# Two DRAM scratch tensors laid out with whole 2 KB rows, their stores split by halves of the partitions

## The chip, the cores and the metric

One NeuronCore of one Trainium2 chip runs the kernel. The metric is device time in microseconds of one launch, as the median of several executions. Each profile is of one execution; its span is the time from the first to the last instruction that the profiler saw.

## The reference, cut to what matters

For a signal `x` of 2048 positions and 512 channels the reference mixes a long convolution (state-space taps `K`, by FFT) and a two-layer MLP with GELU:

```python
g = sigmoid((x * gate_w).sum(-1, keepdims=True))
P = exp(logdA[:, :, None] * l[None, None, :])            # 512 x 128 x 2048
K = einsum("dn,dnl,dn->dl", Cc, P, dB).real              # the taps
y = irfft(rfft(pad(x.T)) * rfft(pad(K)))[:, :2048].T + x * Dskip
b = gelu(x @ w1 + b1) @ w2 + b2                          # F = 1792
return g * y + (1 - g) * b
```

All arrays are float32. The kernel gets `x` in three layouts: `xl` for the transform, `xs` for the gate, `xt` for the MLP.

## The kernel before, in words

The kernel has two stages. The **front** (`front`, lines 347 to 1046) computes the MLP, the taps `K`, and the first step of the Fourier transforms of the signal and of the taps; it lasts until about 406 us. The **convolution stage** (`conv`, lines 1049 to 1233) then finishes the transforms, multiplies them, transforms back and adds everything up.

In the front, TensorE works on three streams. The MLP's products are L870 to L872 (hidden layer, into `ph`, twelve matmuls a block) and L916 to L918 (output layer, into `acc`, three matmuls for each `f`); each product is taken three times, of high and low parts. The taps come in 16 rounds, 4 blocks `u` of channels by 4 parts `c`: VectorE builds powers and rotations (`y`, `xc`), TensorE contracts them (L706), ScalarE copies the result to `s1` (L719), TensorE takes the first transform step (L424, reading `s`), and ScalarE copies that into `sk` (L726). After the fourth part of a block, four DMAs (L745) store `sk` to the DRAM tensor `tk_d`. The signal comes in 16 pieces: a load (L439), the first transform step (L424, reading `attic`), a copy from PSUM (L445 on VectorE for the first three, else L450 on ScalarE) into one of two buffers `st` (a part of `attic`), and a store (L454) of 512 KB to the DRAM tensor `tu_d`.

Both DRAM tensors exist to turn the data: what was stored with frequency and real/imaginary part on the partitions (and channel half `h` on the two halves of the partitions) is read back by `load_u` (L340) and `load_k` (L345) with 64 positions and the two parts on the partitions, and all 512 channels in a row. Each load moves 256 KB; there are 32 of each. Of the `load_u` loads 19 are issued in the front (`early`), the rest and all `load_k` loads in the convolution stage, some steps ahead of their use.

The order of the front is not that of the code. Every step is a task with an engine, an estimated duration, a due time and its reads and writes (`Plan.add`). A planner simulates the engines forwards and backwards 20 times (`Plan.run`), and keeps the order whose simulated end is earliest; the tasks are then issued in that order. The due times come from constants at the head of the file (`K_0`, `D_KA`, `D_S1`, `D_SP`, `D_MAG` and others). So a change of a constant, or of the number of tasks, can move any instruction of the front. DMA tasks go to the SP queue (a few to POOL), which takes them strictly in order: a DMA that waits for its data holds back all DMAs behind it. The `conv` stage has a fixed order.

The convolution stage has 16 steps of about 5.5 us on TensorE: transforms of the taps (`p2k`) and of the signal (`p2u`), both L1090, products on VectorE (L1112 to L1117), and the inverse transform (`pa`, L1129), which goes through DRAM once more (`t4_d`, L1138 and L1147) to the last products `pb` (L1218). Its first step needs a table `cc` (L1062) and the first two `tk` tiles. A `tk` load needs all four last stores of `tk_d`.

Of the kernel before, what the change touches and what calls it, by code (L numbers as in the profile page):

```python
# [9 lines left out]
F32 = mybir.dt.float32  # L10
# [9 lines left out]
D = 512  # L20
# [9 lines left out]
UW = 128  # L30
# [3 lines left out]
NB = 2 * NSB  # L34
T_0 = 19.5
T_MLP = 393.85
K_0 = 27.624
T_KG = 378.228
U_0 = -84.42
U_GAP = 14.351  # L40
LAG = 11.64
D_KA = -51.158
D_KP = -41.862
D_S1 = -7.88
D_EV = -33.69
D_H = -59.76
D_LO = -11.892
N_ACC, N_H, N_IO = 2, 2, 3
D_SP = -9.73
N_LD, N_UX, N_ST = 4, 2, 2  # L50
SCRATCH = 2048
D_XS = 5.631
# [6 lines left out]
W_MLP = (-0.0504, -0.0333, 0.0274)  # L59
W_KG = (-0.054, -0.0194, -0.0114)  # L60
W_U = (-0.0194, -0.1484, 0.0049)
D_MAG = 0.44
D_ROT = 1.203
D_CON = 0.574
D_PHA = 0.94
# [31 lines left out]
def k0_order():  # L97
    return [8 * (n % 4) + n // 4 for n in range(32)]
# [191 lines left out]
def gated_mix(  # L290
# [18 lines left out]
    nc = tc.nc  # L309

    cp = ctx.enter_context(tc.tile_pool(name="cp", bufs=1))
    dr = ctx.enter_context(tc.tile_pool(name="dr", bufs=1, space=DRAM))

    dt_d = dr.tile([1, D], F32, name="dt_d")
    t4_d = dr.tile([4, 2, 2, GROUP, 32, D], F32, name="t4_d")
    tu_d = dr.tile([2, 32, 2, 64, D // 2], F32, name="tu_d")
    tk_d = dr.tile([2, 32, 2, 64, D // UW, 64], F32, name="tk_d")


    ov = out.rearrange("(m i) p d -> m (i p) d", i=2).rearrange("m (p i) d -> m p i d", i=2)  # L320
# [10 lines left out]

        return [attic[:, k] for k in range(N_ATTIC)] + [loft[:, k * D : k * D + D] for k in range(N_LOFT)]

    def halves(z):

        return z.rearrange("p (h e) -> p h e", h=2)

    def load_u(to, n):

        nc.sync.dma_start(halves(to), tu_d[:, k0_order()[n]].rearrange("h c s e -> (c s) h e"))  # L340

    def load_k(to, n):

        of = tk_d[:, k0_order()[n]].rearrange("h c s u e -> (c s) h (u e)")
        nc.sync.dma_start(halves(to), of)  # L345

    def front(pool, psum, keep, attic, loft):

# [17 lines left out]
        def move(kb, fn, due, reads=(), writes=(), queue="SP", after=()):  # L366

            hold = 0.45 if queue == "SP" else 1.0
            return pl.add(queue, hold, fn, due, reads, writes, done=kb / 360.0, after=after)
# [7 lines left out]
        sk = pool.tile([P, 64, NCH, 4, 4], F32, name="sk")  # L377
# [12 lines left out]
        st = [attic[:, 2 * k : 2 * k + 2].rearrange("p a b -> p (a b)").rearrange("p (j e) -> p j e", j=4) for k in range(N_ST)]  # L390
# [38 lines left out]
            mm(1000, products, due + D_S1, [key, "c1"], [("pz", i)], 0.5, switch=True)  # L429
            evac(i)  # L430

        rows = tu_d.rearrange("h k c s e -> (h k c) s e")

        def signal():
            for s in range(16):
                t = U_0 + 16 * U_GAP * warp(s / 16, W_U)
                yield t
                u = s % N_UX
                move(256, lambda s=s, u=u: nc.sync.dma_start(ux[u], xl[s]), t - 10, [], [("ux", u)])  # L439

                def evac(i, s=s, t=t):
                    k = take("st", N_ST)
                    if s < N_SV:
                        vec(
                            4 * 256, lambda: nc.vector.tensor_copy(st[k], pq[i]), t + D_EV,  # L445
                            [("pz", i)], [("st", k)],
                        )
                    else:
                        act(
                            4 * 256, lambda: nc.scalar.copy(st[k], pq[i]), t + D_EV,  # L450
                            [("pz", i)], [("st", k)],
                        )
                    move(
                        512, lambda: nc.sync.dma_start(rows[:, 4 * s : 4 * s + 4], st[k]), t,  # L454
                        [("st", k)], [("u_d", s)],
                    )

                first_stage(lambda r, h, u=u: ux[u][r, 256 * h : 256 * h + 256], ("ux", u), t, evac)
            yield None

        def early():

            us = places(attic, loft)
            keys = [("st", k // 2) for k in range(2 * N_ST)] + [("ux", k) for k in range(N_UX)]
            keys = [*keys, *(("ld", k) for k in range(N_LD)), "gwb"]
            yield 1e6
            for n in range(N_US):
                if n < N_ATTIC:
                    due, key = T_EARLY + 4 * n, [keys[n]]
                else:  # L470
                    due, key = T_LOFT + n, ["xt", "xv"] if n < N_ATTIC + 4 else ["tt"]
                move(
                    256, lambda n=n: load_u(us[n], n), due,
                    [("u_d", k) for k in range(16)], key,
                )
            yield None

# [151 lines left out]
        def waves(t):  # L629
# [4 lines left out]

            act(99 * CW, sines, t + D_KA, ["ph"], ["tt"], "sin", ops=3)

# [18 lines left out]
        e = y[:, 1]  # L655
# [40 lines left out]
        def contract(u, c, k, t):  # L696
# [42 lines left out]
                [("sk", i) for i in range(NCH)],  # L739
            )  # L740
            for h in range(4):
                ss = slice(h * 16, h * 16 + 16)

                def store(ss=ss):
                    nc.sync.dma_start(  # L745
                        tk_d.rearrange("h k c s u e -> (h k c) s u e")[:, ss, u],
                        sk[:, ss].rearrange("p s c j g -> p s (c j g)"),
                    )

                move(700, store, t + 5, [("sk", i) for i in range(NCH)], [])  # L750

        def taps():
# [3 lines left out]
            nth = 0  # L756
            t = K_0
            yield t
# [7 lines left out]
            for g in range(nc_ * NCH):  # L766
                u, c = divmod(g, NCH)
                k = nth % 2
                t = K_0 + T_KG * warp(g / (nc_ * NCH), W_KG)
                yield t  # L770
# [267 lines left out]
        while heap:  # L1038
            heap.sort(key=lambda e: e[:2])
            _, n, s = heap.pop(0)  # L1040
            t = next(s)
# [270 lines left out]
```

## Time and profile before

| what | value |
|---|---|
| median of 3 runs | 535.32 us (534.39 to 537.9) |
| the profiled execution | 536.27 us, span 534.5 us, mean granted TensorE clock 0.979 |
| TensorE (PE) busy | 503.5 us, 94% of the span |
| VectorE (DVE) busy | 426.6 us, 80% |
| ScalarE (ACT) busy | 358.6 us, 67% |
| DMA packets | 90837, 108.61 MB |
| of these under 512 B / under 2 KB | 39056 / 58576 |

Rows of the profile read as follows. A group has source line, engine, operation, `output<-inputs` by the program's tile names, partitions x elements, count, then busy time and the mean of one in ns, and last the idle time of the engine just before these instructions with the one that ended it. A row of a timeline has its start and its length in us. A row of the waits has who waited for whom: us in total, times, longest. A row of a table by windows has, for a stretch `A:B`, the busy us and the count of each engine, then the granted TensorE clock (PEclk, 1.00 is full), the mean busy share of the 16 DMA engines, and what they moved in GB/s. A row of DMA issues has count, KB each and the median us from issue to landing.

### The profile page before, as it was taken

To read this page: it belongs to the slowest core of one execution; us is meant where nothing else is said; L and a number is where in the kernel's file an instruction comes from. 1 tells how busy PE (TensorE), PEld (TensorE's weight loads), DVE (VectorE), ACT (ScalarE), POOL (GpSimd) and SP (SyncE) were. 2 spreads that over 40 slices of the span, in tenths; PEclk is the share of its full clock that TensorE was granted. 3 is DMA by queue.
4 is the path that set the end of the run, shared out by engine and by line. 5 is a ranking of instruction groups with operands and counts; after the bars stand their busy time and mean duration, and the time that the engine had idled before them with its cause. 6 is when DMAs were issued, how large, how long until landed. Compare 5 with 4: busy or idle time off the path is not lost.

```text
span 534.5 us, 11251 instructions
## 1 busy us (share of the span) xinstructions
PE 503.5 (94%) x4426; PEld 352.9 (66%) x4426; DVE 426.6 (80%) x790; ACT 358.6 (67%) x547; POOL 47.3 (9%) x90
## 2 busy tenths in 40 slices
PE   7979999999999799999999999999994899999992
PEld 4757778788777577888788877788783433333360
DVE  5998999989999789999998899997610567666533
ACT  5799887699966898976388968566532454555311
POOL 1000000000000020003110311041001001010103
PEclk9989999999999899999999999999998799999997
DMA  8998923462299269438820547075409979999877
GB/s 254 371 340 308 340 86 117 140 221 66 80 289 304 84 215 279 149 99 219 195 42 2 159 86 152 1 178 89 131 6 217 306 252 312 359 414 385 311 282 288
DMA packets 90837, 108.61 MB, mean 203 GB/s; under 512 B 39056, under 2 KB 58576, under 8 KB 90144
## 3 DMA queue, kind: packets, MB, share of 16 engines
q1 hardware_dynamic: 82944, 87.67, 49.7%
q0 software_dynamic: 7360, 18.65, 14.2%
q10 hardware_dynamic: 480, 1.57, 0.8%
q8 instruction: 35, 0.57, 0.5%
q14 instruction: 18, 0.15, 0.1%
HBM read 62.25 MB, written 45.62 MB: 202 GB/s over the span
## 4 chain that ended last, share of the span: by engine, by line
PE 66%; DVE 11%; DMA 9%; ACT 5%; issue 4%; SPq 2%; POOL 1%; POOLq 0%; DVEq 0%; ACTq 0%
PE pz L706 9%; PE ph L870 7%; PE ph L871 7%; PE ph L872 7%; PE acc L916 6%; PE acc L917 6%; PE acc L918 6%; PE p2k L1090 6%; PE p2u L1090 6%; PE pa L1129 5%; DMA out_dram<-io 2%; PE pz L424 2%; DMA cc<-in_c_dram 1%; DVE y L670 1%; SPq L745 1%
## 5 line engine op out<-in xcount | busy, mean ns | idle before, releaser
L870 PE MATMUL ph<-xh,wh 128*128 128x512 f32 x224 | 90.1, 402 | 0.0
L916 PE MATMUL acc<-wh,hh 128*128 128x512 f32 x210 | 86.0, 410 | 3.4 <-ACT acc L922 2.8
L871 PE MATMUL ph<-xlo,wh 128*128 128x512 f32 x224 | 87.9, 392 | 0.5 <-DVE xlo L804 0.5
L872 PE MATMUL ph<-xh,wl 128*128 128x512 f32 x224 | 87.6, 391 | 0.0
L917 PE MATMUL acc<-wl,hh 128*128 128x512 f32 x210 | 82.7, 394 | 0.0
L918 PE MATMUL acc<-wh,hl 128*128 128x512 f32 x210 | 82.6, 393 | 0.0
L706 PE MATMUL pz<-y,xc 128*32 128x64 f32 x2048 | 61.8, 290 | 5.2 <-ACT attic L450 5.2
L889 ACT ACTIVATE io<-ph,b1t 128x512 f32<-128x512 f32 x56 | 38.6, 689 | 39.2 <-PE ph L872 30.4
L706 PEld LDWEIGHTS pz<-y,xc 128*32 128x32 f32 x2048 | 57.1, 136 | 11.5 <-ACT attic L450 6.1
L898 DVE TENSOR_TENSOR hl<-io,hh 128x512 fp32r<-128x512 f32 x56 | 38.4, 685 | 24.6 <-ACT hh L890 24.6
L916 PEld LDWEIGHTS acc<-wh,hh 128*128 128x128 f32 x210 | 39.7, 189 | 20.1 <-issue 7.1
L870 PEld LDWEIGHTS ph<-xh,wh 128*128 128x128 f32 x224 | 42.3, 189 | 13.8 <-issue 3.8
L871 PEld LDWEIGHTS ph<-xlo,wh 128*128 128x128 f32 x224 | 42.4, 189 | 9.5 <-DVE xlo L804 0.9
L872 PEld LDWEIGHTS ph<-xh,wl 128*128 128x128 f32 x224 | 42.3, 189 | 9.2
L918 PEld LDWEIGHTS acc<-wh,hl 128*128 128x128 f32 x210 | 39.8, 190 | 8.8
L670 DVE TENSOR_TENSOR y<-y,ea 128x64 f32<-128x64 f32 (+4 forms) x80 | 45.2, 565 | 0.4
L1112 DVE TENSOR_TENSOR v<-p2u,k 128x512 f32<-128x512 f32 x16 | 11.1, 691 | 42.5 <-ACT sa L1135 25.3
L917 PEld LDWEIGHTS acc<-wl,hh 128*128 128x128 f32 x210 | 40.0, 190 | 7.5
L515 DVE TENSOR_TENSOR loft<-xc,zz 128x256 f32<-128x256 f32 (+2 forms) x48 | 37.1, 772 | 0.6 <-ACT xc L641 0.5
L516 DVE TENSOR_TENSOR loft<-xc,zz 128x256 f32<-128x256 f32 (+2 forms) x48 | 37.0, 771 | 0.0
L683 DVE TENSOR_TENSOR y<-y,loft 128x2048 f32<-128x2048 f32 x16 | 36.6, 2284 | 0.6 <-ACT loft L633 0.5
L890 ACT CAST hh<-io 128x512 fp32r<-128x512 f32 x56 | 34.8, 622 | 1.8
(139 smaller groups left out, 842.1 us busy)
## 6 DMA issues: line engine op xcount, KB each, us to landing
tu_d<-attic SPq DMA_DIRECT2D x16, 512.0 KB, 4.9
tk_d<-sk SPq DMA_DIRECT2D x16, 512.0 KB, 6.9
tk<-tk_d SPq DMA_DIRECT2D x32, 256.0 KB, 4.9
t_d<-sa SPq DMA_DIRECT2D x31, 256.0 KB, 5.3
t<-t_d POOLq DMA_DIRECT2D x12, 512.0 KB, 7.0
attic<-tu_d SPq DMA_DIRECT2D x22, 256.0 KB, 4.4
attic<-in_xt_dram SPq DMA_DIRECT2D x16, 256.0 KB, 4.1
attic<-in_xl_dram SPq DMA_DIRECT2D x16, 256.0 KB, 4.3
```

Of the source, the lines that this page charges most:

```text
L515: vec(2 * m, lambda: vv.tensor_mul(t, a, br), due, [ka, *kb], [kt])
L670: nc.vector.tensor_mul(both(n, 64 - 3 * n, n), both(0, 64 - n, n), an)
L706: nc.tensor.matmul(pk[32 * j : 32 * j + 32, gg // 4, gg % 4], x[:, r, :, ch], y[:, r, :, ch], start=(r == 0), stop=(r == 1), skip_group_ch ...
L870: nc.tensor.matmul(phs[q], h, xh[d], start=(d == 0), stop=False)
L871: nc.tensor.matmul(phs[q], h, xlo[d], start=False, stop=False)
L872: nc.tensor.matmul(phs[q], lo, xh[d], start=False, stop=(d == 3))
L889: nc.scalar.activation(g, phs[q], AF.Gelu_apprx_tanh, bias=b1t[:, c : c + 1])
L898: SB, lambda: nc.vector.tensor_sub(hl[f], g, hh[f].bitcast(F32)), t + D_LO,
L916: nc.tensor.matmul(a, h, wh[1][f], start=(f == 0 and u >= NSB), stop=False, skip_group_check=True)
L917: nc.tensor.matmul(a, h, wl[1][f], start=False, stop=False, skip_group_check=True)
L918: nc.tensor.matmul(a, l, wh[1][f], start=False, stop=(f == FH - 1), skip_group_check=True)
L1090: nc.tensor.matmul(out[64 * i : 64 * i + 64], w, x, start=True, stop=True)
```

## The change

`tu_d` and `tk_d` get the channel half `h` as an inner dimension instead of the outermost one. In DRAM the two halves of one row (1 KB each) now lie side by side. A load takes 128 contiguous rows of 2 KB instead of 256 pieces of 1 KB. The store of a signal piece, in which `h` lies on the partitions, is now two DMAs of 64 partitions and 256 KB each instead of one of 128 partitions and 512 KB; in DRAM its pieces are 1 KB, every 2 KB, where four of them lay together as 4 KB before. The four stores of a taps block stay four DMAs of 512 KB with pieces of 256 B; each now takes 64 partitions by 32 rows instead of 128 by 16. Five constants of the planner change as well.

```diff
-K_0 = 27.624
+K_0 = 27.09
-D_KA = -51.158
+D_KA = -46.527
-D_S1 = -7.88
+D_S1 = -8.01
-D_SP = -9.73
+D_SP = -13.612
-D_MAG = 0.44
+D_MAG = 0.439
...
-    tu_d = dr.tile([2, 32, 2, 64, D // 2], F32, name="tu_d")
-    tk_d = dr.tile([2, 32, 2, 64, D // UW, 64], F32, name="tk_d")
+    tu_d = dr.tile([32, 2, 64, 2, D // 2], F32, name="tu_d")
+    tk_d = dr.tile([32, 2, 64, 2, D // UW, 64], F32, name="tk_d")
...
     def load_u(to, n):
-        nc.sync.dma_start(halves(to), tu_d[:, k0_order()[n]].rearrange("h c s e -> (c s) h e"))
+        nc.sync.dma_start(to, tu_d[k0_order()[n]].rearrange("c s h e -> (c s) (h e)"))
     def load_k(to, n):
-        of = tk_d[:, k0_order()[n]].rearrange("h c s u e -> (c s) h (u e)")
-        nc.sync.dma_start(halves(to), of)
+        nc.sync.dma_start(to, tk_d[k0_order()[n]].rearrange("c s h u e -> (c s) (h u e)"))
...
-                    move(
-                        512, lambda: nc.sync.dma_start(rows[:, 4 * s : 4 * s + 4], st[k]), t,
-                        [("st", k)], [("u_d", s)],
-                    )
+                    for h in range(2):
+                        def store(h=h):
+                            to = tu_d[:, :, 4 * s : 4 * s + 4, h].rearrange("k c s e -> (k c) s e")
+                            nc.sync.dma_start(to, st[k][64 * h : 64 * h + 64])
+                        move(256, store, t, [("st", k)], [("u_d", s, h)])
...
             for h in range(4):
-                ss = slice(h * 16, h * 16 + 16)
-                def store(ss=ss):
+                a, ss = h % 2, slice(h // 2 * 32, h // 2 * 32 + 32)
+                def store(a=a, ss=ss):
                     nc.sync.dma_start(
-                        tk_d.rearrange("h k c s u e -> (h k c) s u e")[:, ss, u],
-                        sk[:, ss].rearrange("p s c j g -> p s (c j g)"),
+                        tk_d[:, :, ss, a, u].rearrange("k c s e -> (k c) s e"),
+                        sk[64 * a : 64 * a + 64, ss].rearrange("p s c j g -> p s (c j g)"),
                     )
```

The planner gives another order for the whole front; the order of the convolution stage is the same. Line numbers from the front on are 4 to 7 lower in the changed kernel.

**SP, the first store of a signal piece.** On the SP queue, before (`xh_d` and `xl_d` are stores of the MLP's split input, `in_xl_dram` is the signal's load):

```order
L439 DMA attic<-in_xl_dram 128x512
L830 DMA xh_d<-xh_105 128x512
L830 DMA xl_d<-xlo_106 128x512
L830 DMA xl_d<-xlo_108 128x512
L454 DMA tu_d<-attic 128x1024
L830 DMA xl_d<-xlo_107 128x512
L830 DMA xl_d<-xlo_109 128x512
```

and the same place now:

```order
L432 DMA attic<-in_xl_dram 128x512
L826 DMA xh_d<-xh_104 128x512
L826 DMA xl_d<-xlo_106 128x512
L826 DMA xl_d<-xlo_107 128x512
L450 DMA tu_d<-attic 64x4x256 x2
L826 DMA xl_d<-xlo_108 128x512
L826 DMA xh_d<-xh_105 128x512
L826 DMA xl_d<-xlo_109 128x512
```

One store has become two, at nearly the same place in the queue.

**ACT, the first presets of the output accumulator.** `acc` starts from a copy of `b2b`, the broadcast bias (its load now stands earlier on SP, ahead of the last weights). On ACT, before (the `xc` and `ea` rows are the exponentials of the first taps block):

```order
L890 CAST hh_143<-io_154 128x512
L556 ACTIVATE loft<-pr 128x128 x7
L563 ACT_TABLE_LOAD
L563 ACTIVATE ea_96<-pr 128x128 x6
L563 ACTIVATE xc_91<-pr 128x128 x5
L922 COPY acc_84<-b2b 128x512
L579 ACTIVATE loft<-loft 128x768
```

and now:

```order
L798 CAST wh_120<-sk 128x512
L918 COPY acc_84<-b2b 128x512
L918 COPY acc_85<-b2b 128x512
L885 ACTIVATE io_152<-ph_87,b1t 128x512
L886 CAST hh_141<-io_152 128x512
L798 CAST wh_122<-y 128x512
```

The two presets stood behind the exponentials; they now stand ahead of the fourth block's GELU, and the exponentials come later.

**PE, the end of the front.** The last round of the taps ends with the transform step `pz<-s_101` (x8: eight in a row). On PE, before:

```order
L870 MATMUL ph_86<-xh_105,wh_115 128x512
L871 MATMUL ph_86<-xlo_109,wh_115 128x512
L872 MATMUL ph_86<-xh_105,wl_129 128x512
L424 MATMUL pz<-s_101,c1t 64x256 x8
L916 MATMUL acc_84<-wh_120,hh_141 128x512
L917 MATMUL acc_84<-wl_134,hh_141 128x512
L918 MATMUL acc_84<-wh_120,hl_148 128x512
L870 MATMUL ph_87<-xh_102,wh_116 128x512
```

and now:

```order
L419 MATMUL pz<-s_101,c1t 64x256 x8
L912 MATMUL acc_84<-wh_119,hh_140 128x512
L913 MATMUL acc_84<-wl_133,hh_140 128x512
L914 MATMUL acc_84<-wh_119,hl_147 128x512
L912 MATMUL acc_85<-wh_119,hh_140 128x512
L913 MATMUL acc_85<-wl_133,hh_140 128x512
L914 MATMUL acc_85<-wh_119,hl_147 128x512
L866 MATMUL ph_86<-xh_102,wh_115 128x512
```

Between this step and the first matmul of the convolution stage stood 36 MLP matmuls; 54 stand there now. The block of twelve that ends in the first three rows before (`ph_86`, `wh_115`) and six output matmuls (`wh_119`) went behind it. The first contraction L706 of the taps moved the other way: 204 MLP matmuls stood ahead of it, 222 stand there now. The total is the same.

More of the change, by code (lines that the diff above doesn't have):

```diff
@@ L332, in places @@
         return [attic[:, k] for k in range(N_ATTIC)] + [loft[:, k * D : k * D + D] for k in range(N_LOFT)]
-    def halves(z):
-        return z.rearrange("p (h e) -> p h e", h=2)
     def load_u(to, n):
-        nc.sync.dma_start(halves(to), tu_d[:, k0_order()[n]].rearrange("h c s e -> (c s) h e"))
+        nc.sync.dma_start(to, tu_d[k0_order()[n]].rearrange("c s h e -> (c s) (h e)"))
     def load_k(to, n):
-        of = tk_d[:, k0_order()[n]].rearrange("h c s u e -> (c s) h (u e)")
-        nc.sync.dma_start(halves(to), of)
+        nc.sync.dma_start(to, tk_d[k0_order()[n]].rearrange("c s h u e -> (c s) (h u e)"))
     def front(pool, psum, keep, attic, loft):
@@ L430, in first_stage @@
             evac(i)
-        rows = tu_d.rearrange("h k c s e -> (h k c) s e")
         def signal():
@@ L473, in early @@
                     256, lambda n=n: load_u(us[n], n), due,
-                    [("u_d", k) for k in range(16)], key,
+                    [("u_d", k, h) for k in range(16) for h in range(2)], key,
                 )
```

## The prediction, made before the changed kernel was run

> **What bounds the kernel now.** I read the slices of the whole span first, then TensorE's waits, then the chain of waits around the seam between the two stages, and the DMA rows last. The slices, 13.4 us each:
>
> ```profile
> PE   7979999999999799999999999999994899999992
> DVE  5998999989999789999998899997610567666533
> PEclk9989999999999899999999999999998799999997
> DMA  8998923462299269438820547075409979999877
> ```
>
> TensorE is busy nearly throughout. It dips in slice 14 (174 to 187 us) and in slices 31 and 32 (401 to 428 us), and there the granted clock dips too. VectorE is nearly as full until slice 28. DMA is full at the start and again from 428 us. TensorE's waits over the whole run, the longest ones:
>
> ```profile
> PE p2k L1090 <- ACT f L1075: 9.2, 1, 9.2
> PE pz L706 <- ACT attic L450: 5.2, 3, 3.1
> PE acc L916 <- ACT acc L922: 2.8, 1, 2.8
> ```
>
> So in the front TensorE loses 2.8 us once and 5.2 us in three pieces; the 9.2 us lie at the seam.  The chain of waits through the seam (start, length, what):
>
> ```profile
> 398.58 1.02 ACT sk L726
> ...
> 399.62 0.36 SPq L745
> ...
> 400.02 1.32 SPq L745
> ...
> 401.39 2.78 SPq L745
> ...
> 404.27 2.34 SPq L745
> ...
> 406.72 8.01 DMA cc<-in_c_dram
> ...
> 414.75 0.41 ACT f L1074
> ...
> 415.59 4.23 PE p2k L1090 x8
> ```
>
> The last copy into `sk` ends at 399.6; the four stores of the last taps block follow on SP, then the `cc` table, which lands behind them, and TensorE starts the convolution at 415.6. Two timeline rows complete it: TensorE's last front matmul, and the first `tk` loads, which go out only when the stores have landed.
>
> ```profile
> 405.96 0.39 PE L918 MATMUL acc<-wh,hl 128*128 128x512 f32 x1
> 412.59 1.90 SPq L345 DMA_DIRECT2D tk<-tk_d  x4
> ```
>
> The seam is therefore a race with two lanes: from the last `sk` copy to the first product it takes 16.0 us (415.6 - 399.6), and TensorE has MLP work for only 6.7 us of it (to 406.3). Behind the seam TensorE is full, with the DMA near its limit beside it:
>
> ```profile
> 440.00:460.00 20.00, 20.00 (x90) 6.40 (x88) 13.73 (x23) 10.88 (x24) 2.09 (x4) 1.00 0.96 317
> 460.00:480.00 20.00, 20.00 (x90) 6.37 (x89) 12.72 (x22) 10.30 (x21) 2.04 (x4) 1.00 1.06 399
> 512.00:514.00 2.00, 2.00 (x10) 1.69 (x9) 0.27 (x1) 0.00 (x0) 0.00 (x0) 1.00 0.01 2
> ```
>
> **The loads.** 64 loads change from 256 pieces of 1 KB to 128 of 2 KB. The nearest rows are loads of the same 256 KB that already have 2 KB rows:
>
> ```profile
> tk<-tk_d SPq DMA_DIRECT2D x32, 256.0 KB, 4.9
> attic<-tu_d SPq DMA_DIRECT2D x22, 256.0 KB, 4.4
> attic<-in_xt_dram SPq DMA_DIRECT2D x16, 256.0 KB, 4.1
> attic<-in_xl_dram SPq DMA_DIRECT2D x16, 256.0 KB, 4.3
> ```
>
> That is 0.1 to 0.8 us of landing per load. In the convolution stage it earns nothing: TensorE has no wait on a load there (20.00 of 20.00 busy in both rows above), and at 512 us, ahead of the last turn through DRAM, the DMA is idle (share 0.01), so no backlog is carried into the tail. The cover is TensorE's own work; if it were gone, the loads would set the pace, and lighter ones would help. On the path lie only the first two `tk` loads at the seam. They are issued together, so I take half of the 0.8 us once: **-0.4 us**, bounds 0 and -1.6 (both in full).
>
> **The stores of the taps.** Same four DMAs, bytes and 256 B pieces per block, but 64 partitions each, and twice the distance in DRAM between pieces. The last burst before, by 2 us:
>
> ```profile
> 402.00:404.00 2.00, 2.00 (x11) 1.65 (x10) 0.69 (x1) 0.93 (x2) 0.00 (x0) 1.00 0.90 214
> 404.00:406.00 2.00, 2.00 (x11) 1.61 (x9) 0.00 (x0) 0.69 (x1) 0.00 (x0) 1.00 0.89 214
> 406.00:408.00 2.00, 0.35 (x2) 0.00 (x0) 0.00 (x0) 0.69 (x1) 1.42 (x2) 1.00 0.89 213
> ```
>
> 4 x 512 KB at 214 GB/s are 9.8 us. No row of the trace has a large transfer from half the partitions. Bounds: nothing changes, or only half the rate is reached, 9.8 us more; a gain of more than 0.5 us is excluded, since the pieces stay as small. I take **+0.5 us**, near the burst's own row, because piece size and engine share (0.89) are what it shows as the limit.
>
> The Trainium skill (page "SBUF — State Buffer", section on the DMA port swizzle) says that 64 adjacent partitions reach 8 of 16 ports at about 27.2 GB/s each, and the section after it that two transfers of one half each do not add up. That ceiling, 218 GB/s, is an estimate from the page; it lies just above the 214 GB/s of the rows, so by it this burst stays as it is, while the signal's stores would slow down (a rival below).
>
> **The stores of the signal.** 16 stores of 512 KB become 32 of 256 KB with 1 KB pieces in DRAM. The rows of before:
>
> ```profile
> tu_d<-attic SPq DMA_DIRECT2D x16, 512.0 KB, 4.9
> ...
> L454 SPq DMA_DIRECT2D tu_d<-attic x16: 319/326/2371, 25.4 to 194.5; - x16
> ```
>
> 16 more issues of 0.33 us (the median of the second row, which gives ns) are 5.3 us of SP over 170 us, and what is queued behind each (signal loads, `xh_d`, `out_dram`) goes out 0.33 us later. The landing is late by less than one more store's 4.9 us; there are two `st` buffers, and a piece comes every 11 us (169 us / 15), so a buffer has that long to empty. The cover is that pause, and I cost this at **0**. If it is gone, ScalarE waits for `st`, and TensorE for ScalarE, as in the 5.2 us above.
>
> **The new order, at the seam.** 18 more MLP matmuls stand behind the last transform of the taps. Their pace is in the chain of waits:
>
> ```profile
> 394.81 0.23 PE ph L871
> ```
>
> 18 x 0.23 = 4.1 us. If TensorE reaches the end of its MLP work at the same time as before (the total is unchanged), the last `sk` copy, the stores and the start of the convolution are all **4.1 us** earlier, and TensorE idles about 5 us instead of 9.2. The clock's dip moves along with the pause: I cost it at no change. Bounds: -4.1, and 0 if TensorE meets new waits of that size ahead.
>
> **The new order, in the front.** The wait of 2.8 us belongs to these rows:
>
> ```profile
> 32.82 0.57 ACT L922 COPY acc<-b2b 128x512 f32<-128x512 f32 x1
> 33.45 0.50 PE L916 MATMUL acc<-wh,hh 128*128 128x512 f32 x1 [2.76 <-ACT acc L922]
> 34.32 0.63 PE L916 MATMUL acc<-wh,hh 128*128 128x512 f32 x1
> 20.00:40.00 20.00, 17.24 (x108) 12.39 (x106) 18.28 (x39) 17.66 (x39) 0.54 (x1) 0.91 1.01 359
> ```
>
> The preset stood behind the exponentials; it now stands ahead of them, so this wait goes. After it the clock fell (0.91 over 20 us, so 3.6 us at half, worth 1.8 us). Together up to 4.6 us. But what is late next is VectorE, which has the taps to build:
>
> ```profile
> 0.00:100.00 100.00, 93.22 (x753) 68.19 (x754) 90.00 (x186) 80.27 (x123) 3.39 (x13) 0.98 0.72 248
> 100.00:200.00 100.00, 95.79 (x1100) 76.63 (x1099) 92.55 (x180) 85.99 (x121) 4.40 (x12) 0.98 0.57 181
> 200.00:300.00 100.00, 100.00 (x944) 80.71 (x943) 96.74 (x174) 76.43 (x124) 12.79 (x26) 1.00 0.53 139
> ```
>
> VectorE idles 20.7 us in 300. The first contraction now stands 18 matmuls later on TensorE and the last one 18 earlier, so between them 8.2 us fewer are left, and VectorE's idle time must shrink by as much. I therefore take **-1.0 us** of the 4.6; bounds -4.6, and +4.1 if VectorE can give nothing and eats the gain at the seam.
>
> **Sum.** -0.4 + 0.5 + 0 - 4.1 - 1.0 = -5.0 us on the profiled execution, whose time is 536.27 (span 534.5 and 1.8 around it): 531.3. The median of the runs is 0.95 below that execution, so on the scale of the median **530.3 us**. One per cent, about what a measurement of this kernel can tell from no change, is 5.4 us; the bound is 530.0.
>
> **Rivals.**
>
> *The order gives all it can* (0.15). The wait of 2.8 us and its clock dip go in full, and the three waits of 5.2 us shrink by half. -0.4 + 0.5 - 4.1 - 4.6 - 2.6 = -11.2: 524. For it: these waits follow from DMA landings and ScalarE's order, which the new order changes. Against: VectorE's idle time of 7%.
>
> *Nothing arrives* (0.17). VectorE is the bound: the last `y` is ready no earlier, TensorE waits for it, and what stands behind the last transform is done later instead. The rows for and against:
>
> ```profile
> 382.20 1.22 DVE L694 TENSOR_TENSOR y<-y,loft 128x1024 f32<-128x1024 f32 x1
> ...
> 389.23 3.76 PE pz L706 x116
> ```
>
> The last `y` was ready at 383.4 and used at 389.2, 5.8 us later; so 4.1 us fit, but only if VectorE is not late itself. Then -0.4 + 0.5: 535.4.
>
> *Half the partitions, half the rate* (0.18), the slower side. The taps burst at the seam takes up to 9.8 us longer, and the first burst, near 155 us, delays the output stores behind it on SP, for which ScalarE already waits:
>
> ```profile
> L889 ACT ACTIVATE io<-ph,b1t 128x512 f32<-128x512 f32 x56 | 38.6, 689 | 39.2 <-PE ph L872 30.4 <-DMA out_dram<-io 8.4
> ```
>
> I add 3 us for that, about a third of the longer burst. -0.4 - 4.1 - 1.0 + 9.8 + 3 = +7.3: 542.6. It decides against the change from about 150 GB/s down (2.1 MB in 14 us, +4.2, which eats the 4.1). For it: pieces of both halves no longer mix in one DMA. Against: the burst's limit looks like the small pieces, not the place they come from.
>
> By the skill's port ceiling, beside this rival, the signal's 8.4 MB would take 38 us of transfer at 218 GB/s instead of some 23 at the 359 GB/s of the row from 20 to 40 us, an estimate; most of it would be hidden where the DMA's share is 0.5.
>
> **How the numbers follow.** The forecast has 0.50, its own range 527.5 to 533; it lies half below 530.0. Faster by over 1%: 0.25 + 0.15 = 0.40. Within 1%: 0.25 + 0.17 = 0.42. Slower: 0.18. The range 525 to 540 leaves out most of the first and last rival, about 2 in 10.
>
> **What would show it.** Right: the convolution's first `p2k` starts at 410 to 412 us with an idle time of 4 to 6 us ahead of it; `acc` no longer waits near 31 us; the burst still moves 200 GB/s or more at 256 B; DMA packets fall by 8192 - 6144 = 2048 to about 88800 (loads 64 x 128 fewer, signal stores 16 x 384 more); from the first product to the end the time is as before, 534.5 - 415.6 = 118.9 us. Wrong: TensorE's waits for `y` or `attic` grow by more than 3 us in the front; ScalarE waits for stores of `tu_d`; the last burst takes over 12 us.

## The result, and the profile after

The changed kernel is slower: 554.29 us in the median against 536.47 us for the kernel before, measured beside it. The ratio is 1.0335, with a 95% interval of 1.0307 to 1.0363. The prediction was 530.3 us (525 to 540). The sign was wrong, and the time lies above the range. What came is nearest to the rival that had 0.18, half the partitions and half the rate, though the rate fell by less than half and the price was higher than that rival had put down.

The profiled execution took 554.03 us, with a span of 552.3 us: 17.8 us more than the 534.5 before. The slices of the whole span, 13.8 us each:

```profile
PE   9999999999998779999579999989996599999992
PEclk9999999999999799999879999999999699999997
```

Before, TensorE dipped near the start (slices 1 and 3), in slice 14, and at the seam. Now it dips in slices 13 to 15, again in slices 20 and 21, and at the seam (31 and 32), and the clock goes down with it. TensorE's longest waits in the changed kernel:

```profile
PE p2k L1086 <- DMA tk<-tk_d: 9.8, 1, 9.8
PE pz L702 <- ACT sk L722: 9.5, 1, 9.5
PE ph L866 <- ACT io L885: 6.1, 2, 4.1
PE pz L702 <- ACT attic L443: 4.1, 2, 3.0
```

The wait at the seam, 9.2 us before, did not shrink to about 5; it is 9.8. And two long ones are new: 9.5 us for `sk`, and 6.1 us for `io`. TensorE's work in the front ended at 406.30 before, and ends at 433.55 - 9.80 = 423.75 now (the start of the first product, two fences below, less its wait). Two rows by windows, of before and of the changed kernel, tell where these 17.4 us come from:

```profile
0.00:406.30 406.30, 394.71 (x3870) 310.40 (x3870) 358.75 (x681) 307.87 (x445) 33.32 (x72) 0.99 0.57 167
```

```profile
0.00:423.75 423.75, 396.79 (x3870) 310.37 (x3870) 357.19 (x681) 305.67 (x443) 33.28 (x72) 0.98 0.58 161
```

The same 3870 matmuls keep TensorE busy 2.1 us longer, at a lower mean clock, and it idles 27.0 us instead of 11.6. So 15.4 of the 17.4 us are new idle time in the front. The convolution stage is no part of the loss: from the first product to the end it takes 552.3 - 433.55 = 118.8 us, against 118.9 before.

The seam in the changed kernel, by three rows of its timeline: the issue of the last four stores of the taps, the first loads behind them, and the first product.

```profile
412.93 9.99 SPq L741 DMA_DIRECT2D tk_d<-sk  x4
...
429.57 1.75 SPq L340 DMA_DIRECT2D tk<-tk_d  x4
...
433.55 2.65 PE L1086 MATMUL p2k<-tk,cc 128*64 128x512 f32 x4 [9.80 <-DMA tk<-tk_d]
```

The order did what the prediction said: TensorE's front work now ends 423.75 - 412.93 = 10.8 us after the stores are issued, instead of 406.30 - 399.62 = 6.7, which is the 4.1 us. But the first load goes out 16.6 us after the stores, not 13.0 (412.59 - 399.62). While the burst runs, the rows by 2 us read (the last two columns are the DMA engines' busy share and GB/s):

```profile
416.00:418.00 2.00, 2.00 (x11) 1.64 (x10) 0.69 (x1) 0.92 (x2) 0.00 (x0) 1.00 0.79 163
418.00:420.00 2.00, 2.00 (x11) 1.64 (x10) 0.00 (x0) 0.94 (x2) 0.00 (x0) 1.00 0.79 169
420.00:422.00 2.00, 2.00 (x10) 1.66 (x9) 0.69 (x1) 0.37 (x1) 0.00 (x0) 1.00 0.86 178
422.00:424.00 2.00, 1.75 (x8) 1.13 (x6) 0.00 (x0) 0.90 (x2) 0.38 (x1) 1.00 0.68 142
424.00:426.00 2.00, 0.00 (x0) 0.00 (x0) 0.00 (x0) 0.48 (x1) 1.33 (x2) 1.00 0.85 182
```

That is 142 to 182 GB/s at a busy share of 0.68 to 0.86, where the same bytes in the same 256 B pieces had 214 GB/s at 0.89 to 0.90 before. The engines that move the data stand idle more of the time, which speaks against them as what holds the burst back. The DMA rows say the same of the stores, and speak of the loads too (the last column is the median from issue to landing). The stores before, then the rows of the changed kernel:

```profile
tk_d<-sk SPq DMA_DIRECT2D x16, 512.0 KB, 6.9
```

```profile
tk_d<-sk SPq DMA_DIRECT2D x16, 512.0 KB, 9.4
tk<-tk_d SPq DMA_DIRECT2D x32, 256.0 KB, 5.2
attic<-tu_d SPq DMA_DIRECT2D x22, 256.0 KB, 4.6
```

Taps stores land after 9.4 us instead of 6.9. The loads of whole 2 KB rows land no sooner than those of 1 KB pieces did before (4.9 and 4.4 us). The place in the middle where TensorE waits for `sk` shows in one row each of ScalarE's timeline; before:

```profile
265.00 1.01 ACT L726 COPY sk<-pz 128x1024 f32<-128x1024 f32 x1 [7.36 <-DMA tk_d<-sk]
```

and in the changed kernel, with TensorE's row behind it:

```profile
278.46 1.01 ACT L722 COPY sk<-pz 128x1024 f32<-128x1024 f32 x1 [11.11 <-DMA tk_d<-sk]
...
279.52 3.82 PE L702 MATMUL pz<-y,xc 128*32 128x64 f32 x128 [9.50 <-ACT sk L722]
```

There is one `sk`. These are the ninth of its 16 copies: the first copy of the third block has to wait until the stores of the second have read `sk` out. Before, ScalarE waited 7.4 us for that and TensorE had other work; now ScalarE waits 11.1 us and TensorE 9.5 of them.

### The profile page after: what moved, and what is told of

The parts are those of the page before. It is cut to its first block, busy times and chain, and to the rows that moved or that the text cites. A ratio compares the mean times of both kernels' runs of the same rounds, so it can differ in the third digit from the quotient of the medians.

```text
span 552.3 us, 11273 instructions
## 1 busy us (share of the span) xinstructions
PE 505.4 (92%) x4426; PEld 351.3 (64%) x4426; DVE 425.0 (77%) x790; ACT 356.4 (65%) x545; POOL 47.2 (9%) x90
## 2 busy tenths in 40 slices
DMA packets 89044, 108.60 MB, mean 197 GB/s; under 512 B 39312, under 2 KB 50640, under 8 KB 88352
## 4 chain that ended last, share of the span: by engine, by line
PE 50%; DVE 18%; ACT 14%; DMA 11%; issue 4%; SPq 1%; DVEq 0%; ACTq 0%
PE pz L702 6%; PE pa L1125 6%; PE p2k L1086 5%; PE p2u L1086 5%; PE ph L866 4%; PE ph L867 4%; PE ph L868 4%; PE acc L912 4%; DMA tk_d<-sk 4%; PE acc L913 3%; PE acc L914 3%; DMA out_dram<-io 3%; DVE loft L512 2%; DVE loft L511 2%; DVE y L679 2%
## 5 line engine op out<-in xcount | busy, mean ns | idle before, releaser
L1108 DVE TENSOR_TENSOR v<-p2u,k 128x512 f32<-128x512 f32 x16 | 11.1, 691 | 42.7 <-ACT sa L1131 25.3
L926 ACT ACTIVATE io<-acc,gate 128x512 f32<-128x512 f32 x30 | 20.3, 684 | 33.5 <-PE acc L914 32.7
```

## The experiments

The change does three things at once: another order of the front, other rows in DRAM, and stores that each read 64 neighbouring partitions. The first four runs take these apart. Four theories stood against each other: (A) the way out of SBUF, 64 neighbouring partitions give up their data more slowly than 128; (B) the new order; (C) the distances in DRAM; (D) the shape of the transfer, 64 partitions by 32 rows. Ratios are to the kernel before, run beside each version on the same chip.

**The order alone.** The changed kernel's constants and order, with the old rows, and stores from all 128 partitions (the signal's store still in two DMAs, of two rows each):

```diff
-    tu_d = dr.tile([32, 2, 64, 2, D // 2], F32, name="tu_d")
-    tk_d = dr.tile([32, 2, 64, 2, D // UW, 64], F32, name="tk_d")
+    tu_d = dr.tile([2, 32, 2, 64, D // 2], F32, name="tu_d")
+    tk_d = dr.tile([2, 32, 2, 64, D // UW, 64], F32, name="tk_d")
...
-    to = tu_d[:, :, 4 * s : 4 * s + 4, h].rearrange("k c s e -> (k c) s e")
-    nc.sync.dma_start(to, st[k][64 * h : 64 * h + 64])
+    to = tu_d.rearrange("h k c s e -> (h k c) s e")
+    nc.sync.dma_start(to[:, 4 * s + 2 * h : 4 * s + 2 * h + 2], st[k][:, 2 * h : 2 * h + 2])
...
-    tk_d[:, :, ss, a, u].rearrange("k c s e -> (k c) s e"),
-    sk[64 * a : 64 * a + 64, ss].rearrange("p s c j g -> p s (c j g)"),
+    tk_d.rearrange("h k c s u e -> (h k c) s u e")[:, ss, u],
+    sk[:, ss].rearrange("p s c j g -> p s (c j g)"),
```

> The changed kernel's order of every instruction, with the layout of before: both scratch tensors with the channel half outermost, all stores over 128 partitions (a signal piece still goes in two DMAs of 256 KB, each 128 partitions by two rows). Theory A (the stores of half the partitions are slow, and the front's new waits follow from them): the last taps burst moves about 214 GB/s again, the wait of TensorE behind the copy into sk (9.5 us) is under 3 us, and the time is 529 to 534 us, below before, as the forecast had it without its stores. Rival B (the new order itself makes the waits): the burst is fast again, but the time stays at 546 us or more.

Measured: 538.94 us, ratio 1.0046 (1.002 to 1.0072). The order is not the loss, but it is no gain either, and theory A's number for this run, a gain, missed, as did rival B's 546 us. Its longest waits on TensorE, and one window of its last burst:

```profile
PE pz L702 <- ACT sk L722: 6.6, 1, 6.6
PE p2k L1086 <- DMA tk<-tk_d: 5.2, 1, 5.2
```

```profile
404.00:406.00 2.00, 2.00 (x10) 1.64 (x10) 0.69 (x1) 0.00 (x0) 0.00 (x0) 1.00 0.90 215
```

The burst is back at 215 GB/s, and the wait at the seam fell from 9.2 to 5.2 us, the 4 us of the prediction. A new wait of 6.6 us for `sk`, which theory A had put under 3 us, has taken them back.

**The layout alone**, in the order of before: new rows, stores from 64 neighbouring partitions, the old constants.

> The order of before on every engine, with the changed layout and the stores by halves of the partitions (each signal store is two DMAs, one right behind the other). Theory A: the four taps bursts are some 3 to 5 us longer each, the last one's 4.6 us at the seam are paid in full, and the time is 545 to 554 us. Rival B: only the seam's 4 to 5 us are paid: 539 to 542 us.

Measured: 549.89 us, ratio 1.026 (1.0205 to 1.0315). Most of the loss comes without the new order, and the time is what theory A expected. TensorE's longest waits in that run:

```profile
PE p2k L1090 <- DMA tk<-tk_d: 14.9, 1, 14.9
PE pz L706 <- ACT attic L448: 10.8, 3, 8.7
```

The seam waits 14.9 us instead of 9.2, and the signal's copies (`attic`) hold TensorE for 10.8 us instead of 5.2.

**Halves in the old rows.** The order of the changed kernel and the old DRAM tensors, but each store from 64 neighbouring partitions:

```diff
-    tk_d.rearrange("h k c s u e -> (h k c) s u e")[:, ss, u],
-    sk[:, ss].rearrange("p s c j g -> p s (c j g)"),
+    tk_d[a, :, :, ss, u].rearrange("k c s e -> (k c) s e"),
+    sk[64 * a : 64 * a + 64, ss].rearrange("p s c j g -> p s (c j g)"),
```

(the signal's stores likewise).

> The changed kernel's order, the layout of before, but all stores by halves of the partitions: 64 neighbouring partitions, with the DRAM rows as far apart as before (1 KB for the taps, 4 KB in one piece for the signal). Theory A1 (64 neighbouring partitions are what is slow): the last burst moves 165 to 180 GB/s, the time is 550 to 556 us. Rival C (the double distance between pieces in DRAM is what is slow): the burst moves 205 GB/s or more, and the time is that of the kernel with the order alone, 529 to 534 us.

**Every other partition.** The same order, tensors and shape of the taps' stores, 64 partitions by 32 rows, but every other partition instead of 64 neighbours; the signal is stored from all 128:

```diff
-    tk_d[a, :, :, ss, u].rearrange("k c s e -> (k c) s e"),
-    sk[64 * a : 64 * a + 64, ss].rearrange("p s c j g -> p s (c j g)"),
+    tk_d[:, :, a, ss, u].rearrange("h k s e -> (h k) s e"),
+    sk[a:P:2, ss].rearrange("p s c j g -> p s (c j g)"),
```

> The changed kernel's order, the layout of before; each taps store takes 64 partitions by 32 rows as in the changed kernel, but every other partition (real or imaginary parts) over all 128 instead of 64 neighbours; the signal's stores take all 128. Theory A1 (which partitions, so the way out of SBUF): the burst moves about 214 GB/s, the time is 529 to 534 us. Rival D (64 partitions by 32 rows as a shape, wherever they lie): the burst moves 165 to 180 GB/s, and the time is 545 us or more.

Measured: 550.35 us, ratio 1.025 (1.0204 to 1.0297), with neighbours; 539.64 us, ratio 1.0046 (1.0018 to 1.0075), with every other partition. One window of the last burst each, first with neighbours, then with every other:

```profile
410.00:412.00 2.00, 2.00 (x11) 1.65 (x10) 0.69 (x1) 0.94 (x2) 0.00 (x0) 1.00 0.78 162
```

```profile
404.00:406.00 2.00, 2.00 (x10) 1.65 (x9) 0.69 (x1) 0.63 (x2) 0.00 (x0) 1.00 0.89 213
```

With neighbours the time is the one that theory A1 expected (A, with neighbouring partitions as what is slow). With every other partition A1's rate came, but its time, 529 to 534 us, did not: the order alone has no such gain either. Old rows with neighbours are slow, so the new distances in DRAM (C) aren't needed for most of the loss. The same shape with every other partition is fast, so the shape (D) isn't the cause. What is left of the four is A: which partitions a store reads. A direct comparison follows below.

**Taps or signal.** The changed kernel with only one of the two tensors changed, the other with old rows and stores from all 128 partitions. First the taps changed, then the signal changed.

```diff
 # the taps alone: the signal's tensor, its loads and stores are the old ones
-    tu_d = dr.tile([32, 2, 64, 2, D // 2], F32, name="tu_d")
+    tu_d = dr.tile([2, 32, 2, 64, D // 2], F32, name="tu_d")
 # the signal alone: the taps' tensor, its loads and stores are the old ones
-    tk_d = dr.tile([32, 2, 64, 2, D // UW, 64], F32, name="tk_d")
+    tk_d = dr.tile([2, 32, 2, 64, D // UW, 64], F32, name="tk_d")
```

> The changed kernel, but only the taps keep the new rows and the stores by 64 neighbouring partitions; the signal is stored whole and in halves of DRAM, as before. Theory S (the seam: the loss is the taps' last burst, and the waits for sk behind the third one): 550 to 554 us, the landing of the stores of tk_d near 9 us, first p2k near 432 us. Theory G (the signal: its pieces of 1 KB cost most, taken up by transfers that they push back): 541 to 545 us. Theory B2 (each its share): 546 to 549.

> The changed kernel, but only the signal keeps the new rows and the stores by 64 neighbouring partitions; the taps are stored from all 128 partitions, as before. Theory S: 539 to 540.5 us, as the run with the order alone (538.9), since the signal's buffers st rest long enough. Theory G: 549 to 553 us, with waits for attic or io of 4 us more than there. Theory B2: 542 to 545.

Measured: taps 550.34 us, ratio 1.0281 (1.0253 to 1.031); signal 543.27 us, ratio 1.0134 (1.0107 to 1.0162). Against the order alone (1.0046) the taps cost 2.35%, 12.6 us, and the signal 0.88%, 4.7 us. The order's 0.46%, 2.5 us, makes it 19.8; the whole change measured 3.35%, 18.0 us, so the parts nearly add up. Theory S (the loss is the taps' bursts) has the taps' number, but had called the signal free, and that was wrong; the signal's number lies in the range of theory B2 (each its share). TensorE's longest waits in the run with the taps alone:

```profile
PE p2k L1086 <- DMA tk<-tk_d: 10.9, 1, 10.9
PE pz L702 <- ACT sk L722: 8.2, 1, 8.2
PE ph L866 <- ACT io L885: 5.0, 3, 4.1
```

The place of the signal's loss shows on the SP queue. The last pieces are stored close together; before, three in 6.1 us, and with the order alone three in two parts each, still from 128 partitions, in 7.9 us:

```profile
188.71 6.13 SPq L454 DMA_DIRECT2D tu_d<-attic  x3
...
186.45 7.88 SPq L450 DMA_DIRECT2D tu_d<-attic  x6
```

In the run with the signal alone the three pieces go in two halves each. The rows show these stores, followed by the ScalarE copy that waits for them and TensorE's product that waits for it:

```profile
187.64 11.95 SPq L450 DMA_DIRECT2D tu_d<-attic  x6
...
197.32 1.01 ACT L443 COPY attic<-pz 128x1024 f32<-128x1024 f32 x1 [4.70 <-DMA tu_d<-attic]
...
198.39 2.02 PE L702 MATMUL pz<-y,xc 128*32 128x64 f32 x64 [6.05 <-ACT attic L443]
```

The queue needs 12 us for them, ScalarE waits 4.7 us for a buffer, and TensorE 6.0 us for ScalarE (2.4 us at this place with the order alone). In the changed kernel TensorE's longest wait for `attic` is 3.0 us.

**New rows without neighbours.** The changed kernel, and then the kernel before with only the layout, each with stores from every other partition. The two channel halves are thereby mixed in the scratch, and the output's values are other ones; number, size and targets of all transfers are those of the changed kernel.

```diff
-    nc.sync.dma_start(to, st[k][64 * h : 64 * h + 64])
+    nc.sync.dma_start(to, st[k][h:P:2])
...
-    sk[64 * a : 64 * a + 64, ss].rearrange("p s c j g -> p s (c j g)"),
+    sk[a:P:2, ss].rearrange("p s c j g -> p s (c j g)"),
```

> The changed kernel, with whole rows and stores from 64 partitions still, but from every other partition instead of 64 neighbours; the two channel halves are thereby mixed in the scratch, so the values of the output are other ones and the work is the same. If the neighbours are the whole cause: 538 to 540 us (the order alone had 538.9), and the landing of tk_d's stores 7.5 to 8 us. If the whole rows cost something of their own (1 KB pieces of the signal, other distances in DRAM), as the 4 us between the changed kernel and the run with halves in old rows suggest: 542 to 545 us. If the whole rows earn something on the load side: below 537.

> The kernel before in its own order, with whole rows and stores from every other partition (the channel halves mixed in the scratch, the work the same). The whole rows alone, without the neighbours and without the new order. If whole rows earn what I had put down for them (0.4 us): 535 to 536.5 us, no difference. If they cost something of their own: 539 to 541. If they earn more than I had seen: below 533, and then a correct form of it is worth building.

Measured: 539.80 us, ratio 1.008 (1.0054 to 1.0107), in the new order; 537.49 us, ratio 1.0041 (1.002 to 1.0061), in the old one. The first is what was expected of neighbours as the whole cause; the second lies between two of its ranges. The first is also the sharpest of all these comparisons: its stores write the same DRAM addresses, in the same pieces and the same sequence, as those of the changed kernel (1.0335), and only the partitions that they read from differ. Its last burst:

```profile
404.00:406.00 2.00, 2.00 (x10) 1.65 (x10) 0.69 (x1) 0.00 (x0) 0.00 (x0) 1.00 0.90 215
```

So about 2.5 of the 3.35% are the neighbours; in the old order the same comparison gives 2.2% (1.026 against 1.0041). The second run is the value of whole rows with split stores: not a gain of 0.4 us, but a loss of 0.4%, 2.2 us. In its profile the wait at the seam is 10.5 us instead of 9.2, and the first `tk` load goes out 14.5 us after the stores instead of 13.0. Why that is so wasn't followed further; the signal's stores in pieces of 1 KB are another candidate, which the last run below touches.

**How the neighbours cost.** Three forms of the run with the taps alone (1.0281): both stores of one half of the partitions first and then both of the other, instead of by turns; each store from 32 neighbouring partitions by all 64 rows; and the stores of partitions 64 to 127 on ScalarE's queue, the others on SP's.

```diff
 # one half after the other
-    a, ss = h % 2, slice(h // 2 * 32, h // 2 * 32 + 32)
+    a, ss = h // 2, slice(h % 2 * 32, h % 2 * 32 + 32)
 # quarters
-    a, ss = h % 2, slice(h // 2 * 32, h // 2 * 32 + 32)
-    tk_d[:, :, ss, a, u].rearrange("k c s e -> (k c) s e"),
-    sk[64 * a : 64 * a + 64, ss].rearrange("p s c j g -> p s (c j g)"),
+    a, ss = h % 2, slice(h // 2 * 16, h // 2 * 16 + 16)
+    tk_d[ss, :, :, a, u].rearrange("k c s e -> (k c) s e"),
+    sk[64 * a + 2 * ss.start : 64 * a + 2 * ss.stop].rearrange("p s c j g -> p s (c j g)"),
 # two queues
-    nc.sync.dma_start(
+    (nc.scalar if a else nc.sync).dma_start(
```

> The run with the taps alone (550.3 us), with the four stores of a block in another sequence: both of partitions 0 to 63 first, then both of 64 to 127, instead of by turns. If each half of the partitions has its own way out, and the stores by turns overlap enough at their ends to use some of the other half's (which would be why the burst moved 163 to 178 GB/s and not half of 214): the overlap between the halves is rarer, the burst is 16 to 19 us instead of 14, and the time 553 to 558. If the limit belongs to one store, whichever partitions it reads: 549 to 551.5.

> The run with the taps alone (550.3 us), with each of the four stores of a block from 32 neighbouring partitions (all 64 rows of them) instead of 64. If the rate goes with how many partitions one store reaches at a time: the rate falls further, 555 to 565 us, the landing of tk_d's stores over 11 us. If the four stores of a block overlap so far that their partitions add up: 545 to 551. If 64 neighbours and 32 share the same limit: 549 to 552.

> The run with the taps alone (550.3 us), with the stores of partitions 64 to 127 issued on ScalarE's queue instead of SP's, so that the two halves can run side by side. If each half has its own way out and the two add up: the burst is back at 10 to 11 us, the time 540 to 543 (ScalarE issues 8 DMAs more, some of them in front of work that TensorE waits for). If it is a limit of the transfers themselves, or of where they land: 549 to 553.

Measured: 547.93 us, ratio 1.0226 (1.0183 to 1.0268), one half after the other; 549.65 us, ratio 1.0239 (1.0186 to 1.0292), with quarters; 546.59 us, ratio 1.0186 (1.015 to 1.0222), with two queues. For the first, both ranges of the expectation were missed: the time is not worse than by turns. The burst did get longer, as the idea of two ways out asks. The issue of the last four stores and the first loads behind them, by turns and then one half after the other:

```profile
407.94 9.97 SPq L741 DMA_DIRECT2D tk_d<-sk  x4
...
424.07 1.84 SPq L340 DMA_DIRECT2D tk<-tk_d  x4
```

```profile
403.56 9.87 SPq L741 DMA_DIRECT2D tk_d<-sk  x4
...
421.28 1.77 SPq L340 DMA_DIRECT2D tk<-tk_d  x4
```

From the one to the other it takes 16.1 us by turns and 17.7 us one half after the other. The time does not show it: TensorE's wait at the seam is 10.9 us in both profiles, and in the front it waits less here (3.2 us for `io` instead of 5.0). The windows of this burst, while two stores of the same half run one after the other, and two windows on:

```profile
406.00:408.00 2.00, 2.00 (x10) 1.65 (x9) 0.39 (x1) 1.31 (x2) 0.00 (x0) 1.00 0.71 153
408.00:410.00 2.00, 2.00 (x11) 1.64 (x10) 0.30 (x1) 0.34 (x1) 0.00 (x0) 1.00 0.72 155
410.00:412.00 2.00, 2.00 (x11) 1.65 (x10) 0.69 (x1) 0.96 (x2) 0.00 (x0) 1.00 0.79 162
412.00:414.00 2.00, 2.00 (x11) 1.64 (x9) 0.00 (x0) 0.69 (x1) 0.00 (x0) 1.00 0.79 170
```

One half alone starts with 153 to 155 GB/s, and rises no higher than 170 in these rows. The stores by turns of the changed kernel had 142 to 182. The time of the quarters lies in two of its three ranges at once, the one for partitions that add up and the one for a common limit. Two windows of quarters, and then two of two queues; the first row of each is the first full window of its burst:

```profile
412.00:414.00 2.00, 2.00 (x10) 1.64 (x9) 0.69 (x1) 1.09 (x2) 0.00 (x0) 1.00 0.72 147
414.00:416.00 2.00, 2.00 (x11) 1.64 (x10) 0.00 (x0) 0.77 (x2) 0.00 (x0) 1.00 0.84 182
```

```profile
408.00:410.00 2.00, 2.00 (x11) 1.64 (x9) 0.00 (x0) 0.00 (x0) 0.00 (x0) 1.00 0.97 185
410.00:412.00 2.00, 2.00 (x10) 1.68 (x9) 0.11 (x1) 1.31 (x2) 0.00 (x0) 1.00 1.10 224
```

With 32 partitions the burst starts at 147 GB/s, little below the 153 of 64; the next window, in which stores of both halves can run, has 182. The Trainium skill (page "SBUF — State Buffer", section on the DMA port swizzle) states just this: partitions 0 to 63 reach no more ports than 0 to 31. By its table of ports every other partition reaches all 16, and the rates of 213 to 215 GB/s above agree.

With two queues the halves run side by side, and for 2 us the rate is 224 GB/s, a little over the 213 to 215 that 128 partitions had. The Trainium skill (same page, section "Can I just issue two DMAs to hit both halves?") says that two such DMAs serialize, at 6% over a single one; here the windows of 185 and 224 GB/s are 20 and 45% over the 154 of one half, so for these small pieces the measurement differs from the page. Of the time less than half came back: from 1.0281 to 1.0186, where the order alone has 1.0046. Two rows of its timeline, and the same two of the order alone, tell why:

```profile
405.92 2.94 SPq L741 DMA_DIRECT2D tk_d<-sk  x2
...
420.94 1.78 SPq L340 DMA_DIRECT2D tk<-tk_d  x4
```

```profile
399.96 7.00 SPq L741 DMA_DIRECT2D tk_d<-sk  x4
...
411.47 2.01 SPq L340 DMA_DIRECT2D tk<-tk_d  x4
```

From the issue of the stores to the first `tk` load it is 15.0 us with two queues, 11.5 with 128 partitions, and 16.1 by turns on one queue (rows above): the high rate lasts only for a part of the burst. Both ranges expected, 540 to 543 and 549 to 553, were missed.

**The signal's pieces.** The order alone, with the signal's stores from 64 neighbouring partitions into the old rows, in pieces of 4 KB:

```diff
-    to = tu_d.rearrange("h k c s e -> (h k c) s e")
-    nc.sync.dma_start(to[:, 4 * s + 2 * h : 4 * s + 2 * h + 2], st[k][:, 2 * h : 2 * h + 2])
+    to = tu_d[h, :, :, 4 * s : 4 * s + 4].rearrange("k c s e -> (k c) s e")
+    nc.sync.dma_start(to, st[k][64 * h : 64 * h + 64])
```

> The order alone (538.9 us), with the signal's stores by 64 neighbouring partitions into the old rows, so in pieces of 4 KB instead of 1 KB; the taps are stored whole. The run with the signal alone, with pieces of 1 KB, had 543.3. If the neighbours alone cost that: 542 to 544.5. If they cost it only together with pieces of 1 KB (the difference of 4 us between the changed kernel and the run with halves in old rows): 538 to 540.5.

Measured: 540.64 us, ratio 1.0077 (1.0051 to 1.0103), just above the second range. Over the order alone that is 0.3%, with intervals that overlap; with pieces of 1 KB it was 0.88%. But pieces of 1 KB without neighbours, in the changed kernel with every other partition (1.008), also cost 0.3% over the order alone. So each costs about 0.3% by itself, and whether both together cost more than their sum is not shown. The last three signal pieces on the SP queue say that the two add up. With pieces of 1 KB from every other partition, and then with pieces of 4 KB from neighbours:

```profile
186.38 10.45 SPq L450 DMA_DIRECT2D tu_d<-attic  x6
```

```profile
188.62 9.51 SPq L450 DMA_DIRECT2D tu_d<-attic  x6
```

The order alone took 7.9 us for them. The short pieces add 2.6 us and the neighbours 1.6, together 12.1, and the run with both had 12.0. The changed kernel (1.0335) is 0.85% slower than halves in the old rows (1.025), which store the signal from neighbours in pieces of 4 KB; the short pieces are a candidate for that.

## Why the prediction was wrong, point by point

**The stores of the taps** are the step that failed. I had put down +0.5 us, "because piece size and engine share (0.89) are what it shows as the limit". The run with the taps alone showed 12.6 us. A busy share of 0.89 was no proof that the engines were the limit of every form of this store: with neighbours it fell to 0.68 to 0.86 in the changed kernel, and the rate to 142 to 182 GB/s. The estimate from the Trainium skill's ceiling, 218 GB/s and so no change, took the smaller of two limits, as if a way out that allows 218 GB/s left the 214 as they were. Measured, one half gave 153 to 155, so the two limits don't combine in that way. A second fault was the count: I priced the last burst. The kernel has four. At the seam the wait of the run with the taps alone is 10.9 us, 5.7 over that of the order alone; the rest of the 12.6 us lies in the front, where `sk` costs 8.2 instead of 6.6 us, and `io` 5.0 us. By its rows the wait for `io` goes back to the first burst, near 155 us. In the changed kernel ScalarE waits 3.1 us for these stores before its next copy into `sk`, and then 6.0 us for a load of weights, which stands behind them on the SP queue and goes out at 169.5 us (164.9 with the order alone). Its row in the changed kernel, and with the order alone:

```profile
175.93 0.62 ACT L798 CAST wh<-attic 128x512 fp32r<-128x512 f32 x1 [6.04 <-DMA attic<-in_w_dram]
```

```profile
169.62 0.62 ACT L798 CAST wh<-attic 128x512 fp32r<-128x512 f32 x1 [2.06 <-DMA attic<-in_w_dram]
```

Then ScalarE is late with `io`, and TensorE waits for that.

**The stores of the signal.** Put down as 0, with the pause of 11 us per piece as the cover. Measured: 4.7 us. The cover was an average: the last three pieces have no such pause, as the row of before at 188.71 us could have told me. On the SP queue these three went from 7.9 us with the order alone to 12.0. "ScalarE waits for stores of `tu_d`" was among the signs that would show me wrong, and it came.

**The new order at the seam.** The mechanism was right: TensorE's front work behind the stores grew from 6.7 to 10.8 us, and with whole stores the wait fell to 5.2 us, against the 4 to 6 that I had named. The term of -4.1 was lost before that. The bound that I had given as "0 if TensorE meets new waits of that size ahead" is what happened: 6.6 us for `sk`, in a kernel with one `sk` buffer, whose copy waits for the stores of the block before. I had asked only whether VectorE could be ready earlier. In the profiled executions the span of the order alone, 534.4 us, is that of before, 534.5, but this was the fastest of its ten executions; by the timed ratio it is 0.2 to 0.7% slower. "Nothing arrives" was that rival's name, but its cause was another one than VectorE.

**The new order in the front.** -1.0 us of the 2.8 for `acc`. The wait near 31 us is gone, but a later preset, the third, makes TensorE wait near 41 us in the changed kernel; it comes only after ScalarE has read out the finished `acc`:

```profile
42.70 0.50 PE L912 MATMUL acc<-wh,hh 128*128 128x512 f32 x1 [2.31 <-ACT acc L918]
```

So 0.5 of the 2.8 us are left of this gain (2.8 - 2.3).

**The loads.** Put down as -0.4. The landing got no shorter (5.2 and 4.6 us against 4.9 and 4.4). With the order kept it is the same: in the old order 5.2 and 5.3 us with whole rows (stored from every other partition) against 4.9 and 4.4; in the new one 5.7 and 4.6 against 5.8 and 4.6. And whole rows with split stores made the kernel 0.4% slower. The packets, 89044 against the forecast of about 88800, and the 118.8 us behind the first product were as said: the loads aren't a limit there.

**The rival "half the partitions, half the rate"** had 542.6 us. Its price for the taps, 9.8 + 3 = 12.8 us, is nearly the measured 12.6, but that is luck. At the seam, where it had put 9.8, the first `tk` load went out 4.6 us later with the taps alone than with the order alone (16.1 and 11.5 us after the stores), and TensorE's wait grew by 5.7; in the front, where it had put 3, about 7 us were lost. It fell short because it kept the order's gain of 5.1 us where there was a loss of 2.5, and the signal's 0 where there were 4.7. What was held against it, that the burst's limit looks like the small pieces, "not the place they come from", did not hold: the place cost about 2.5%.

Open is why one half gives 154 GB/s at these pieces and not more, why whole rows cost 0.4%, and whether one half after the other is really a little quicker than by turns (1.0226 and 1.0281, with intervals that overlap). None of these versions beats the kernel before.

## What to carry to other kernels

In this kernel a store from 64 neighbouring partitions was another transfer than the same bytes from 128, or from 64 that are spread: count partitions and where they lie, not only bytes, pieces and packets. A busy share near 0.9 said that the engines were nearly full in one form of the transfer; it didn't say that they would be in another. And where a burst reads a tile that has only one buffer, its length can be on the path at every block, not just at the last one: price each of them.

## What was not expected of the hardware

- 256 B pieces left SBUF at 153 to 155 GB/s from one half of the partitions, at 147 from a quarter, and at 213 to 215 from 128 or from every other one, with the DMA engines at a share of 0.71 to 0.72, 0.72 and 0.89 to 0.90.
- The two halves on two queues reached 224 GB/s for 2 us, against 153 to 155 from one half and 213 to 215 from 128 partitions on one queue.
- Loads of 256 KB in rows of 2 KB landed no sooner than in pieces of 1 KB (5.2 against 4.9 us and 5.3 against 4.4 in the old order, 5.7 against 5.8 and 4.6 against 4.6 in the new one).
